# A fused attention and feed-forward kernel: the written-out order of its steps replaced by another, from the 110th step on

## The chip, the cores and the metric

The kernel runs on one core of one Trainium2 chip. The metric is the device time of one execution in microseconds (us); the runs shown give a median of three.

## The reference

Per batch of 8, with 8 heads, 576 rows, head size 64 and 32 memory slots, then a feed-forward layer over all 4,608 rows:

```python
a = softmax(phi, axis=2)                       # over the 576 rows
k_m = einsum('bhsm,bhsd->bhmd', a, k);  v_m = einsum('bhsm,bhsd->bhmd', a, v)
attn = softmax(q @ k_m.T / sqrt(64), axis=-1)  # 576 x 32 per head
x = (attn @ v_m)                               # -> 4608 x 512
out = leaky_relu(x @ w_in, 0.01) @ w_out       # 512 -> 2048 -> 512, float32
```

The two weight matrices lie in memory as float64, the other inputs and the output as float32.

## The kernel before

`v_m` is multiplied into `w_in` ahead of time (a *fold*), so that the feed-forward layer reads the attention weights directly. Products are made of fp16 pairs, high and low part, three matmuls for each product.

The kernel is a dictionary of named steps and a list that says in which order they are issued. The list has 2,188 entries and 2,180 different steps: a few idle products at the start (`z.f`, `z.1`, `z.2`) are run more than once. The list is in two strings, `OPENING` and `LATER`:

```python
    with tc.manual_schedule(engines={ENG.PE, ENG.DVE, ENG.Activation, ENG.Pool, ENG.SP}):
        run(OPENING.split())
        run(LATER.split())
```

Each engine, and the queue of DMAs that SyncE issues, works through its own steps in the order of this list, and a step waits where what it reads is not ready or the buffer that it writes is not free. No step passes an earlier one of its own engine. The names:

- `i0` to `i3`, `o0` to `o3`: quarters of `w_in` and `w_out`. `ld` loads, `h`, `y`, `t` turn 64-bit words into float32, `k` and `l` split into high and low fp16 parts, `s`, `m`, `n` make sums of blocks of `w_out`, `b` sums squares. `ci.1` to `ci.4` and `co.1` to `co.4` derive scales from them; `ci.2`, `co.2` are four small VectorE instructions (lines 494 to 501), `ci.3`, `co.3` one small product each that waits for them (line 507).
- `a0` to `a7`: attention of a batch. `phi`, `kv`, `q0`, `q1` load; `A` and `B` are the softmax over `phi` (`B10`, line 724, subtracts the maximum on VectorE); `C`, `D` make `k_m`, `v_m` and their transposes (`D3` copies the scaled transpose on ScalarE); `Q` transposes queries; `E1` makes scores on TensorE, `E20` to `E23` transpose them on VectorE (line 1120); `S01` to `S08` are the softmax of the scores and its split into fp16 parts, of which `S01` (line 1143), `S02`, `S04` to `S06` and `S08` (line 1207) are VectorE's for batches 2 to 7.
- `Wbj.p` folds quarter j of `w_in` for batch b (line 1242); `h` splits off the high part on ScalarE, `l` the low part on VectorE (line 1281). `w1.1` is `W10.p`.
- `u0` to `u7`: the first 384 rows, in float32: `P` up (line 1340), `V` leaky ReLU on ScalarE, `O` down (line 1411, three products of 512 columns). `P8` to `P15`, with `V`, `C`, `L`, `O`: the next 384 rows, in fp16.
- `p0` to `p59`: the remaining 3,840 rows in 15 groups of 256 rows by four quarters of the hidden size. `p` makes one of four 128 x 256 blocks of the hidden layer (line 1453), two halves of one PSUM bank in turn, so that a `p` step needs the `v` step (leaky ReLU, ScalarE, lines 1472 and 1474) of the block two before. `s` (lines 1488 to 1490) makes four sums of blocks on VectorE; `c.0`, `c.1` cast to fp16 on ScalarE (line 1494), `l.0`, `l.1` make the low parts on VectorE (line 1498). `d.0` to `d.6` are seven products of six matmuls (line 1521); `d.0`, `d.1`, `d.6` read what `l.0` wrote, the other four what `l.1` wrote.
- `x2` to `x15` combine the seven products of a group on VectorE (`x.p` on ScalarE; `x.3` is line 1541), `z` scales and stores, `end` does both for the last group in pieces.

Of the kernel before, what the change touches and what calls it, by code (L numbers as in the profile page):

```python
# [82 lines left out]
o2.m2 o2.s3 V15.0 o2.l2 a3.phi C14 O12.0 V15.1 p0.0 o2.m3 o3.k0 v0.0 o3.k2 O12.1 i2.k1 p0.1 o3.s0
C15 p0.2 L14 O13.0 i3.k1 o3.s1 v0.2 a2.q1 a3.A1 a2.Q1 v0.1 L15 a2.E1 p1.0 i2.l1 o3.s2 o3.l0 a2.E21
a2.E22 o3.k1 p0.3 o3.m0 O13.1 v0.3 o3.l1 v1.0 o2.n2 a2.E20 p1.1 c0.0 o2.n3 i2.k2 a3.A2 a2.D2 o3.l2
a2.D11 o3.n0 p1.2 v1.2 O14.0 v1.1 s0 a2.E3 a2.D4 o3.m3 p1.3 a3.A4 o3.m2 a2.E23 c0.1 O14.1 a2.D5 v1.3
O15.0 l0.0 p2.1 o3.m1 a2.S01 O15.1 c1.0 a2.S02 v2.1 o3.n1 a2.S03 Z1.0 l0.1 o3.n3 p2.0 Z1.2 a2.D6
v2.0 a3.A3 o3.n2 d0.0 d0.1 p2.2 d0.5 a3.kv s1 l1.0 p2.3 a2.S04 Z1.1 c1.1 d0.6 d1.1 d1.0 a3.B10 v2.3
v2.2 i2.l2 p3.0 c2.0 i3.k2 W20.p v3.0 d0.3 l2.0 l1.1 d2.1 p3.1 i3.k0 a2.S05 d0.4 a2.S06 v3.1 d1.5 s2
d1.3 a3.B20 d1.6 p3.3 W20.h0 i3.l0 p3.2 a2.S07 W20.l0 a2.S08 d2.0 d0.2 v3.2 a3.C10 W20.h1 v3.3 c3.0  # L90
d1.4 W20.l1 p4.1 i3.l1 d2.6 c2.1 d1.2 a3.B3 l2.1 v4.1 a3.C2 a3.C30 p4.3 p4.0 d2.3 s3 d2.4 a3.C3k
a3.C31 a4.phi a3.q1 a3.q0 l3.0 v4.0 c3.1 a3.C4 a3.D10 p4.2 W21.p d2.2 l3.1 d2.5 v4.2 v4.3 s4 d3.5
W21.h0 d3.0 W21.h1 W21.l0 c4.0 W21.l1 d3.3 l4.0 p5.1 x2.p W22.p p5.0 c4.1 i3.l2 W22.h1 a3.Q1 W22.h0
# [11 lines left out]
l10.1 s11 v12.1 a4.E1 d10.5 a4.C4 os2 a4.E20 v12.0 p12.3 d8.4 c11.0 d9.4 v12.3 p12.2 l11.0 os3 c11.1
a4.E21 p13.1 d9.6 d10.4 a4.D2 v13.1 a4.E22 a5.A1 v12.2 W32.p p13.3 W32.h0 p13.0 l11.1 d10.6 W32.h1
s12 d11.6 c12.0 d10.2 d9.3 W32.l1 W32.l0 v13.3 v13.0 W33.p p13.2 d10.0 a4.D4 d10.1 d11.0 z3.1 d11.2
a4.D11 c12.1 v13.2 d11.1 a5.A2 l12.1 a4.D5 p14.1 p14.0 l12.0 s13 d10.3 W33.h1 c13.0 a4.E23 v14.0
a5.A4 a5.kv v14.1 W33.l1 d11.3 d11.5 x4.p W33.h0 a4.D6 p14.3 p14.2 x4.0 c13.1 W40.p d11.4 v14.2
l13.0 l13.1 v14.3 W33.l0 W40.h1 c14.0 d12.0 d12.5 p15.1 s14 c14.1 x4.1 a5.A3 x4.2 p15.0 d12.6 v15.1  # L110
d12.3 x4.3 W40.l1 W40.h0 p15.3 l14.1 v15.0 d12.1 d13.1 p15.2 z4.0 os4 v15.2 v15.3 a5.B10 c15.0
a5.B20 d12.2 d13.5 a4.S01 d13.2 p16.1 l14.0 W41.p d13.0 d12.4 v16.1 l15.0 p16.0 d14.0 a4.S02 v16.0
z4.1 a4.S03 d14.2 p16.3 p16.2 d13.6 s15 W41.h0 a4.S04 d13.3 v16.2 d14.1 v16.3 p17.1 c15.1 W40.l0
l15.1 W41.h1 W41.l0 p17.0 v17.1 v17.0 d15.0 d13.4 d14.3 s16 p17.2 d14.4 p17.3 a5.C10 a5.B3 v17.3
v17.2 d14.6 p18.1 c16.1 c16.0 a4.S05 W41.l1 a6.phi l16.0 l16.1 p18.0 d15.2 v18.1 v18.0 c17.0 d14.5
s17 d15.4 a5.C2 x5.p a5.C30 c17.1 d15.1 p18.2 p18.3 d15.5 a4.S06 v18.2 d15.3 x5.0 a4.S07 l17.1 p19.0
# [6 lines left out]
d19.3 d20.0 d19.1 d19.2 v22.1 p22.3 s21 x6.0 c21.0 x6.1 x6.2 c21.1 d19.5 l21.0 W43.p v22.3 a6.A3
a5.D2 v22.2 p23.0 c22.0 x6.3 p23.1 v23.1 d21.0 d20.3 v23.0 d20.5 a5.D4 a5.S01 W43.h1 d20.4 p23.2
l22.0 p23.3 l21.1 v23.2 a5.D11 d20.1 a5.D5 s22 d22.0 p24.0 d20.2 c22.1 v23.3 W43.h0 d20.6 z6.1
W43.l1 c23.0 p24.1 a5.S02 v24.0 d21.2 l22.1 v24.1 d21.4 d22.4 a5.D6 p24.2 v24.2 d21.5 z6.0 d21.6
a5.S03 W50.p p24.3 d22.2 s23 v24.3 d21.1 p25.0 p25.1 c23.1 c24.0 d22.1 l23.0 d23.0 d23.1 a6.B10
l23.1 v25.0 v25.1 p25.3 v25.3 s24 a6.B20 d21.3 d23.2 p25.2 p26.1 v25.2 d22.3 W43.l0 c24.1 x7.p d22.6
# [1606 lines left out]
```

## Time and profile before

| | us |
|---|---|
| median of three runs | 647.3 (645.9 to 648.1) |
| the profiled execution | 647.4 |
| its span, first to last instruction | 645.6 |
| TensorE (PE) busy | 630.3 |
| VectorE (DVE) busy | 529.7 |
| ScalarE (ACT) busy | 402.9 |

[...] "Busy" is the union of the instructions' records. A record of a pipelined matmul is longer than the distance to the next one, so that consecutive records overlap, and a short wait between two matmuls can be hidden by the first one's record.

### The profile page before, as it was taken

The page shows a single profiled execution, that of the slowest core. Times are in us where ns is not written, and L with a number is a line of the kernel's source. Part 1 is how long each engine was busy: PE and PEld are TensorE (multiplying, and loading weights), DVE is VectorE, ACT ScalarE, POOL GpSimd, SP SyncE. Part 2 cuts the span into 40 slices and gives each one's busy share as a digit, 9 for nine tenths or more (in the row PEclk, how much of TensorE's full clock was granted, in tenths as well). Part 3 has the DMA queues.
Part 4 walks back from the last instruction along what each step waited for, and adds up shares of the span by engine and source line. Part 5 has one row for each costly group of instructions (what it writes and reads, how often), then busy time and mean ns, then how long its engine had stood idle before and what let it go on. Part 6 is the DMA issues. An engine that isn't in the chain of part 4 may idle for free.

```text
span 645.6 us, 17428 instructions
## 1 busy us (share of the span) xinstructions
PE 630.3 (98%) x7437; PEld 496.7 (77%) x7437; DVE 529.7 (82%) x841; ACT 402.9 (62%) x699; POOL 14.3 (2%) x34
## 2 busy tenths in 40 slices
...
DMA packets 85404, 61.16 MB, mean 95 GB/s; under 512 B 61648, under 2 KB 68560, under 8 KB 85328
## 3 DMA queue, kind: packets, MB, share of 16 engines
...
q10 hardware_dynamic: 576, 0.56, 0.3%
...
## 4 chain that ended last, share of the span: by engine, by line
PE 52%; DVE 6%; SPq 3%; issue 1%; ACT 1%; DMA 0%; DVEq 0%; ACTq 0%
PE po L1521 27%; PE ph L1453 17%; PE ph L1521 4%; SPq L621 3%; PE pa L1242 2%; DVE arena L1498 1%; DVE arena L986 1%; PE pa L794 1%; DVE r1k L656 1%; PE pa L1044 1%; DVE arena L1488 1%; SPq L1394 0%; DMA arena<-in_q_dram 0%; DVE arena L1489 0%; DVE t L1120 0%
## 5 line engine op out<-in xcount | busy, mean ns | idle before, releaser
L1521 PEld LDWEIGHTS <-arena 128*128 128x128 f16 x2520 | 242.0, 98 | 38.2 <-issue 8.5
L1453 PE MATMUL ph<-a,w_mem 128*128 128x256 f16 (+3 forms) x1656 | 157.0, 243 | 1.0 <-ACT wi L1472 0.7
L1521 PE MATMUL po<-wo,arena 128*128 128x256 f16 x1080 | 139.6, 273 | 1.0 <-DVE arena L1498 0.6
L1521 PE MATMUL po<-arena 128*128 128x256 f16 x1080 | 140.0, 273 | 0.0
L1453 PEld LDWEIGHTS <-w_mem 128*128 128x128 f16 x1656 | 128.6, 98 | 14.8 <-issue 4.6
L1474 ACT ACTIVATE wi<-ph,g_scs 128x256 f32<-128x256 f32 x112 | 53.0, 473 | 82.7 <-PE ph L1453 72.9
L1472 ACT ACTIVATE wi<-ph,g_scs 128x256 f32<-128x256 f32 x112 | 52.9, 472 | 66.1 <-PE ph L1453 64.1
L1498 DVE TENSOR_TENSOR arena<-arena 128x1024 f16<-128x1024 f32 (+1 forms) x58 | 69.9, 1205 | 28.2 <-ACT arena L1494 28.2
L1411 PE MATMUL po<-wo,arena 128*128 128x512 f16 (+1 forms) x240 | 77.1, 467 | 0.8 <-DVE wo L424 0.8
L1494 ACT CAST arena<-arena 128x1024 f16<-128x1024 f32 (+1 forms) x58 | 60.2, 1037 | 21.8 <-DVE arena L1490 17.7
L1498 DVE TENSOR_TENSOR arena<-wi,arena 128x768 f16<-128x768 f32 x56 | 52.9, 948 | 6.0 <-ACT arena L1494 5.9
L1521 PE MATMUL ph<-wo,arena 128*128 128x256 f16 x360 | 48.8, 273 | 0.4 <-DVE arena L1498 0.4
L1494 ACT CAST arena<-wi 128x768 f16<-128x768 f32 x56 | 46.6, 831 | 3.4 <-PE po L1521 2.9
L1488 DVE TENSOR_TENSOR arena<-wi 128x512 f32<-128x512 f32 x56 | 38.5, 687 | 8.5 <-ACT wi L1472 4.3
L1340 PE MATMUL ph<-a,w_mem 128*128 128x192 f16 (+1 forms) x232 | 38.0, 313 | 0.0
L1411 PEld LDWEIGHTS po<-wo,arena 128*128 128x128 f32 x96 | 17.4, 190 | 20.2 <-issue 18.4
L1281 DVE SCALAR_TENSOR_TENSOR w_mem<-pa,w_mem 128x512 f16<-128x512 f32 x40 | 26.9, 681 | 7.0 <-ACT w_mem L1275 7.0
L1242 PE MATMUL pa<-wi,vT 64*32 64x512 f16 (+1 forms) x704 | 29.5, 420 | 0.7 <-DVE w_mem L1281 0.7
L1275 ACT ACTIVATE w_mem<-pa 128x512 f16<-128x512 f32 x40 | 23.1, 598 | 8.1 <-PE pa L1242 2.9
L1490 DVE TENSOR_TENSOR arena<-wi,arena 128x256 f32<-128x256 f32 x56 | 23.8, 425 | 2.0
L1453 PE MATMUL ph<-a,arena 128*128 128x256 f16 (+3 forms) x216 | 24.9, 237 | 0.5 <-ACT wi L1472 0.5
L1489 DVE TENSOR_TENSOR arena<-wi,arena 128x256 f32<-128x256 f32 x56 | 23.8, 425 | 1.9
...
## 6 DMA issues: line engine op xcount, KB each, us to landing
...
```

The costliest lines, as they stand in the source:

```text
L1242: nc.tensor.matmul(pf[g][cols, :], lhs, rhs, start=(n == 0), stop=(n == len(passes) - 1), tile_position=(g * D, hh * M),)
L1281: nc.vector.scalar_tensor_tensor(tiles(t[:, 1]), w(g), ws, tiles(t[:, 0]), ALU.mult, ALU.subtract)
L1340: nc.tensor.matmul(ph[:, t0:t0 + n], lhs, rhs, start=(m == 0), stop=(m == len(seq) - 1))
L1411: nc.tensor.matmul(po, lhs, rhs, start=(f == 0 and m == 0), stop=(f == NQ * NF - 1 and m == len(seq) - 1),)
L1453: nc.tensor.matmul(ph[:, t0:t0 + n], lhs, rhs, start=(m == 0), stop=(m == len(seq) - 1))
L1472: nc.scalar.activation(dst, ph, AF.Prelu, scale=g_sc2n[:, j:j + 1], alpha=1.0 / SLOPE)
L1474: nc.scalar.activation(dst, ph, AF.Prelu, scale=g_sc2[:, j:j + 1], alpha=SLOPE)
L1488: nc.vector.tensor_tensor(gt[:, 0:2], two, gf[:, 1:3], ALU.subtract)
L1489: nc.vector.tensor_tensor(gt[:, 2], gf[:, 1], gt[:, 1], ALU.subtract)
L1494: nc.scalar.copy(dst[:, 0], src)
L1498: nc.vector.tensor_tensor(dst[:, 1], src, dst[:, 0], ALU.subtract)
L1521: nc.tensor.matmul(acc, g[:, x, s, u], rhs, start=(h == 0 and j == 0 and u == 0 and m == 0), stop=(j == NQ - 1 and u == 1 and m == 2), ski ...
```

## The change

The two strings are replaced from their 110th entry on (the first 110 entries, up to `u0.V0 u1.P0`, stay). Both lists hold the same steps, each as often; no step's code changes. The change is described as a new search for an order for 15 whole groups in which dependent operations of an engine are taken to run one behind the other, and loads to land later. The lines that the text below speaks of, in the order of the list; the rest is of the same kind:

```diff
-i1.y0 i1.t0 u0.P1 u1.V0 a0.S11 o0.h0 o0.y0 o0.h1 o1.ld1 i1.h2 i2.ld1 a0.S12 o1.ld2 o0.t0 o0.y1 o0.t1
...
-a1.B10 a0.S16 a1.B20 a1.q0 o0.b o2.t2 u4.V0 o1.b o2.b a1.B3 a1.C10 i3.ld1 a1.Q0 a1.C2 a1.C30 u5.P0
-a1.C31 u2.O1 a1.C4 i3.ld0 a1.Q1 i3.ld2 i3.h1 a1.C3k o3.ld2 a1.D11 i2.b a1.D5 a1.D10 a1.D2 u3.O1
-a1.D4 i3.y1 u4.V1 i3.t1 a1.D3 a1.E1 u5.V0 i3.y0 i3.h0 i3.y2 i3.t0 u4.O0 i3.h2 o3.y2 i3.t2 a1.E22
-u5.P1 a1.E20 i3.b a1.S01 a1.E21 a1.S02 f03.1 ci.1 u5.O0 a2.phi o3.h2 a1.S11 a0.S17 o3.ld1 o3.t2
-u5.V1 o3.y1 a1.S03 ci.2 a2.kv2 a1.S12 a0.S18 o3.h1 u4.O1 a2.A1 a1.S04 a1.S13 o3.t1 ci.3 f03.2 a2.A2
-ci.4 o3.ld0 e. w1.1 o3.h0 o3.y0 W00.h0 a1.S05 a1.S06 o3.t0 u6.P0 u7.P0 a1.S14 W10.h0 u6.V0 o0.s0
-W00.h1 a2.A4 o3.b u7.V0 u6.O0 W00.l0 o0.s1 W00.l1 co.1 a1.S07 W01.h0 a2.A3 a2.B10 co.2 u7.P1 W10.h1
-u6.P1 a2.kv0 co.3 a1.S08 i0.k1
+o0.h0 i1.y2 u1.P1 o0.y0 u1.V0 o0.t0 i1.y0 u0.P1 u0.O0 a0.S11 o0.h1 i1.t0 a0.D2 o1.ld1 i1.h1 o0.y1
...
+a1.C30 a1.C3k a1.D10 i3.ld2 a1.C31 a1.C4 i2.b a1.Q1 u4.P0 a1.D2 i3.h1 a1.D11 i3.y1 a1.D3 u3.O1 a1.D4
+a1.D5 u5.V1 i3.y0 o3.ld2 u4.V0 a1.E1 i3.t1 u4.O0 i3.y2 i3.h0 u5.P0 a0.S16 i3.t0 a1.E20 i3.h2 o3.h2
+a2.phi o3.y2 a1.E21 i3.t2 i3.b o3.ld1 a1.S01 u5.V0 a1.E22 f03.1 o3.ld0 ci.1 a1.S02 f03.2 a1.S11
+o3.t2 a1.S12 a2.A1 a1.S13 u5.O0 a1.S03 w1.1 o3.h1 ci.2 a0.S17 a2.A2 o3.y1 ci.3 a1.S04 ci.4 e. a1.S14
+u6.P0 o3.y0 o3.h0 o3.t1 o3.t0 W00.h1 u7.P0 u4.O1 W10.h0 W00.h0 W00.l1 u6.V0 u6.O0 a1.S05 o0.s0
+W00.l0 o0.s1 a0.S18 W10.h1 a1.S06 o3.b W01.h1 co.1 a1.S07 W10.l1 u7.V0 a1.S15 u6.P1 a2.A4 a1.S08
+W10.l0 W11.p co.2 W01.l1 W01.h0 co.3
...
-d4.2 z2.0 c6.0 a3.E1 s6 a3.E23 a3.E21 p7.3 p7.2 z2.1 a3.E22 v7.3 d4.6 l6.0 c6.1 a3.E20 d5.5 d5.4
-W30.p a4.A3 v7.2 p8.1 a4.B10 l6.1 d5.6 d6.0 c7.0 a3.S01 v8.1 p8.0 s7 W30.h0 W30.l0 c7.1 d5.3 d5.2
...
-d8.5 p11.1 a4.C30 p11.0 d9.0 a4.C31 l9.1 v11.0 a3.S08 v11.1 a4.Q0 c10.0 x3.3 d9.1 s10 l10.0 a4.C3k
-d8.2 p11.2 d9.5 v11.2 d8.6 p12.0 p11.3 z3.0 a4.Q1 a4.D10 d8.3 a5.phi c10.1 v11.3 a4.D3 d9.2 p12.1
...
-a6.A1 a6.A2 a4.S08 a5.E20 d17.4 a5.E21 c20.0 d18.6 a5.E23 d17.5 p21.0 p21.1 d18.4 a5.E22 l19.0 a6.A4
...
-l59.0 d58.0 d59.0 end.p l59.1 d58.2 d57.5 d59.2 d59.3 d59.6 d59.4 d58.5 d59.5 end.0 end.1 d57.1
-d58.1 end.2 end.3 end.z1 d59.1 end.4 end.z2 end.5 end.z0
...
+v3.3 d1.4 a3.C10 W20.l1 c2.1 v3.2 p4.0 p4.1 v4.0 a3.C2 l2.1 i3.l1 a3.C30 i3.k2 s3 v4.1 d2.4
...
+d5.3 a3.E21 d5.4 a3.E23 v7.3 p8.0 c7.0 a3.E20 l7.0 p8.1 W30.p d6.6 c6.1 d7.1 d7.0 a4.kv a4.B20 l6.1
+v8.0 W30.h0 v8.1 p8.3 a3.E22 s7 W30.h1 W30.l1 c7.1 p8.2 v8.3 v8.2 d7.6 c8.0 d5.5 a3.S01 l7.1 d5.2 s8
...
+v11.0 v11.1 d9.0 z3.0 a3.S07 p11.3 p11.2 v11.3 d8.4 l10.0 a4.D10 d9.6 a3.S08 d9.3 v11.2 a4.Q1 p12.0
...
+d20.5 d21.4 v23.3 d20.6 a4.S08 v23.2 p24.0 p24.1 c22.0 W42.h1 l22.0 d21.0 c23.0 c22.1 v24.0 d22.0
...
+d57.0 l58.1 s59 d57.2 c59.0 d58.0 d58.3 d58.4 d58.5 d57.6 l59.0 d59.0 d58.6 d58.2 c59.1 l59.1 d59.2
+d59.4 d59.3 end.p d59.6 end.0 d59.5 end.1 d57.1 end.2 d58.1 d59.1 end.4 end.3 end.z2 end.z1 end.5
+end.z0
```

## Rows read from the trace of the kernel before

**Rows 1.** The page's busy time, share and instruction count of each engine.

```profile
PE 630.3 (98%) x7437; PEld 496.7 (77%) x7437; DVE 529.7 (82%) x841; ACT 402.9 (62%) x699; POOL 14.3 (2%) x34
```

**Rows 2.** Windows: busy us (x instructions) by engine, clock, DMA share, GB/s.

```profile
45.00:100.00 55.00, 53.11 (x448) 26.06 (x447) 46.80 (x91) 47.90 (x74) 8.75 (x8) 1.00 0.63 199
100.00:150.00 50.00, 50.00 (x538) 31.27 (x537) 49.47 (x68) 42.73 (x70) 2.12 (x4) 1.00 0.34 76
150.00:275.00 125.00, 122.25 (x1763) 99.54 (x1760) 120.40 (x194) 75.37 (x137) 0.20 (x2) 1.00 0.39 102
275.00:300.00 25.00, 25.00 (x394) 21.92 (x393) 22.09 (x32) 15.12 (x25) 0.00 (x0) 1.00 0.14 39
300.00:500.00 200.00, 198.60 (x2493) 171.16 (x2490) 166.41 (x263) 115.00 (x211) 0.10 (x1) 1.00 0.29 66
500.00:600.00 100.00, 100.00 (x1099) 88.85 (x1099) 71.21 (x103) 56.40 (x99) 0.00 (x0) 1.00 0.07 17
600.00:645.60 45.60, 41.47 (x380) 36.92 (x378) 23.81 (x36) 18.75 (x33) 0.00 (x0) 1.00 0.14 36
```

**Rows 3.** TensorE's timeline: waits; in brackets idle time before and releaser.

```profile
70.00 1.93 PE L1088 MATMUL pa<-arena,kT 32*32 32x192 f32 x96 [0.74 <-ACT kT L937]
...
92.81 0.38 PE L507 MATMUL pa<-diag,ones 4*128 4x4 f32 x2 [1.08 <-DVE diag L501]
...
154.63 0.33 PE L915 MATMUL pa<-ident,x_v 128*128 128x128 f32 x1 [0.24 <-DVE t L1120]
...
263.89 0.84 PE L1242 MATMUL pa<-wi,vT 64*32 64x512 f16 x23 [0.23 <-DVE w_mem L1281]
...
349.27 0.49 PE L1453 MATMUL ph<-a,arena 128*128 128x256 f16 x3 [0.53 <-ACT wi L1472]
```

**Rows 4.** VectorE's timeline: two instructions of an `s` step, and the next.

```profile
236.48 0.42 DVE L1489 TENSOR_TENSOR arena<-wi,arena 128x256 f32<-128x256 f32 x1
236.94 0.42 DVE L1490 TENSOR_TENSOR arena<-wi,arena 128x256 f32<-128x256 f32 x1
237.28 0.68 DVE L1281 SCALAR_TENSOR_TENSOR w_mem<-pa,w_mem 128x512 f16<-128x512 f32 x1
```

**Rows 5.** Opening, from three views: `u3.O1`; `a2.B10` and `co.2`; folds of batches 0, 1.

```profile
66.52 2.74 PE L1411 MATMUL po<-wo,arena 128*128 128x512 f32 x6
...
89.39 1.96 DVE L724 TENSOR_TENSOR arena<-arena,r1k 128x1152 f32<-128x1152 f32 x1
...
91.28 0.27 DVE L494 TENSOR_REDUCE m<-pa 4x1 f32<-4x128 f32 x1
...
91.94 0.82 DVE L501 TENSOR_SCALAR diag<-ident,m 4x4 f32<-4x4 f32 x1
...
L1242 PE MATMUL pa<-wi,vT 64*32 64x512 f32 x128 | 8.7, 601 | 0.0
```

**Rows 6.** Groups of instructions by form, VectorE: `l`, `a.E2`, `a.S01`.

```profile
L1498 DVE TENSOR_TENSOR arena<-arena 128x1024 f16<-128x1024 f32 x56 | 68.0, 1215 | 28.2 <-ACT arena L1494 28.2
...
L1120 DVE STREAM_TRANSPOSE t<-pa 128x512 f32<-128x512 f32 x12 | 8.3, 700 | 1.3 <-PE pa L1044 1.3
...
281.40 1.34 DVE L1143 TENSOR_REDUCE tm<-t 128x36 f32<-128x1152 f32 x1
```

**Rows 7.** Timelines of TensorE and VectorE: a `d` step, `d9.1`, and `x3.3`.

```profile
243.09 0.82 PE L1521 MATMUL ph<-wo,arena 128*128 128x256 f16 x6
243.75 0.82 PE L1521 MATMUL po<-wo,arena 128*128 128x256 f16 x6
...
246.72 0.65 DVE L1541 TENSOR_TENSOR obs<-obs,po 128x512 f32<-128x512 f32 x1
```

**Rows 8.** Timelines of VectorE and TensorE: `a4.S08` and `p24.0`.

```profile
320.62 1.42 DVE L1207 TENSOR_TENSOR a<-t,a 128x1024 f16<-128x1024 f32 x2
...
346.61 0.49 PE L1453 MATMUL ph<-a,arena 128*128 128x256 f16 x3
```

**Rows 9.** Timeline of the end: the last combination.

```profile
641.51 0.48 DVE L1568 SCALAR_TENSOR_TENSOR obs<-po,scales,obs 128x256 f32<-128x256 f32 x1 [1.02 <-PE po L1521]
```

More of the change, by code (lines that the diff above doesn't have):

```diff
@@ L83 @@
[L83 to L93, printed above, removed]
@@ L105 @@
[L105 to L116, printed above, removed]
@@ L123 @@
[L123 to L128, printed above, removed]
@@ new lines @@
+P8.0 a2.A3 o0.s2 o0.n1 W11.l1 i0.k1 o0.m2 u5.O1 o0.k1 o0.s3 V8.0 o0.n2 o0.k0 W11.l0 o0.l2 a2.kv3
+V9.1 P8.1 o0.l1 a2.kv0 i0.l2 i1.k0 i0.l1 P9.0 o1.s0 o0.m3 u6.O1 W02.h0 o0.n3 V8.1 W02.h1 W02.l0
+o0.l0 V9.0 o1.k2 W12.p W02.l1 o1.l2 C8 C9 o1.s1 o1.m0 P10.0 W12.h0 W12.h1 i1.k1 L8 W12.l1 V10.0
+u7.O1 o1.n0 P10.1 Z0.2 a2.B10 W12.l0 Z0.1 V10.1 Z0.0 C10 L9 o1.m1 i1.l1 o1.n1 o1.k0 P11.0 V11.0
+o1.l0 W13.p o1.s2 P11.1 O8.0 V11.1 C11 W03.h1 W03.h0 P12.1 O8.1 L10 a2.B20 V12.1 P13.1 W03.l1 o1.s3
+P12.0 W03.l0 i1.l0 L11 o1.m2 o1.k1 a1.S16 V12.0 o1.l1 O9.0 o1.n2 W13.h0 i2.k0 W13.l0 o2.k0 a1.S17
@@ new lines @@
+v1.2 O14.0 o3.m0 o3.l2 o3.m3 o3.n0 s0 v1.1 a2.E21 a2.E3 O14.1 p1.3 p2.0 a2.E20 o3.m1 a2.D2 o3.n1
+a2.D11 v1.3 a2.E23 O15.0 o3.n2 a2.S01 v2.0 c0.1 o3.n3 p2.1 a2.S02 c1.0 O15.1 a2.D4 v2.1 i2.l2 d0.0
+l0.1 p2.2 a2.D5 a3.kv p2.3 l1.0 Z1.1 Z1.2 Z1.0 d0.3 i2.l1 a2.D6 a3.B10 a2.S03 d0.5 W20.p s1 v2.2
+v2.3 d0.1 p3.0 a2.S04 i3.k0 p3.1 d0.2 d0.6 c1.1 d1.1 a3.B20 d1.6 l1.1 v3.0 d1.3 d0.4 a2.S05 c2.0
+l2.0 v3.1 a2.S06 d1.0 d2.1 s2 a2.S07 p3.2 i3.l0 d2.0 W20.h0 d1.5 W20.l0 a2.S08 p3.3 d1.2 d2.6 a3.B3
+W20.h1 v3.3 d1.4 a3.C10 W20.l1 c2.1 v3.2 p4.0 p4.1 v4.0 a3.C2 l2.1 i3.l1 a3.C30 i3.k2 s3 v4.1 d2.4
@@ new lines @@
+c9.0 p10.3 d7.5 x3.0 d8.5 s9 a4.C2 c9.1 d8.6 a3.S04 x3.1 v10.0 v10.3 l9.0 x3.2 p11.1 d8.1 p10.2 d8.2
+a3.S05 v10.2 l9.1 d9.1 a3.S06 p11.0 a4.C30 d9.5 d9.2 W31.l1 x3.3 c10.0 s10 d8.3 a4.C3k a4.C31 a5.phi
+v11.0 v11.1 d9.0 z3.0 a3.S07 p11.3 p11.2 v11.3 d8.4 l10.0 a4.D10 d9.6 a3.S08 d9.3 v11.2 a4.Q1 p12.0
+c11.0 p12.1 d10.0 a4.Q0 a4.C4 c10.1 l11.0 a4.D3 v12.0 d10.1 a4.E1 l10.1 a4.E22 v12.1 a4.E20 d11.0
+s11 p12.2 p12.3 d11.1 v12.2 d10.3 d10.6 v12.3 c11.1 c12.0 p13.0 p13.1 a4.E21 v13.1 l12.0 W32.p v13.0
```

177 lines of the change are left out of this document (96 added, 81 removed).

## Prediction

> **What bounds the kernel now.** I read the page's busy times first [rows 1]: TensorE is busy for 630.3 of 645.6 us, VectorE for 529.7, ScalarE for 402.9. So no reordering can give more than TensorE's 15.3 us of idle time and what its records hide, and the question is where that idle time lies. The windows [rows 2] answer it: the first 45 us are ahead of the 110th step and stay as they are; of the rest TensorE is idle for 55.00 - 53.11 = 1.89 us up to 100, 0 up to 150, 2.75 from 150 to 275, 0 up to 300, 1.40 from 300 to 500, 0 up to 600, and 4.13 in the last stretch. In those windows the VectorE column tells why: from 100 to 275 it is idle for only 0.53 + 4.60 us, after 500 for 28.8 of 100.
>
> TensorE's timeline then names the waits [rows 3]: two in 45 to 150 (ScalarE's `a1.D3`, VectorE's chain `co.2`); eight in 150 to 275, of which the first and the last are shown, seven ended by VectorE and one by ScalarE; four small ones after 300. A product's record lasts 0.27 us, but six of them start every 0.66 us, 0.109 apart [rows 7], so a wait hides 0.164 us more than it shows. All that can be won between 45 and 600 us is 1.89 + 2.75 + 1.40 + 14 x 0.164 = 8.3 us. The last stretch is not won by order: TensorE ends, one combination of 0.48 us follows [rows 9], then a store; both orders end with `d59.1`, `end.5` and `end.z0`. The new one issues `end.z2` and `end.z1` together shortly ahead of it; I take nothing for that.
>
> The sum is made against the profiled execution, 647.4 us (span 645.6 and 1.8 around it), which is 0.1 above the median of the runs, 647.3. About 0.3% (1.9 us) is what a measurement here can tell from no change.
>
> **The change part by part.** No instruction is added or removed: the list's 2,188 entries come in another order, each engine and the DMA queue in list order. What is priced is cover: the TensorE work that stands between a step and the TensorE step that needs it.
>
> *Opening.* `a1.E1` stood directly behind `a1.D3` and waited 0.74 us, hidden part included 0.90. Now `u3.O1` stands between, 2.7 us of products [rows 5], so the wait goes: -0.9. `co.3` waited 1.08 because `a2.B10` (1.96 us) held up `co.2` on VectorE [rows 5]. `a2.B10` now comes later, but `co.2` (91.28 to 92.76, 1.48 us) stands behind the fold `W11.p`, and nothing of TensorE stands behind that before `co.3`. A fold of this batch is 8.7 / 8 = 1.09 us, so 0.39 of the wait stays: -0.7. `ci.3` loses the `u4.O1` that covered `ci.2` and gets the same place behind the fold `w1.1`: +0.4. Together -1.2; the bounds are -2.2 (1.89 + 2 x 0.164, every wait of this stretch) and +1.5 (neither saving comes, and `ci.3` waits for the whole of its chain).
>
> *150 to 275 us.* Here I counted, in both orders, what VectorE has ahead of the same TensorE step. Ahead of `p8.0` the new order has dropped `a3.E20` (0.70), `l6.1` (1.22) and `a3.S01` (1.34) [rows 6], with nothing of VectorE put in: 3.3 us less. Ahead of `p12.0` VectorE's work is the same, but six more product steps (`d9.2 d8.3 p11.3 d8.4 d9.6 d9.3`), 6 x 0.66 = 3.9 us, stand there for TensorE. So VectorE gets 3 to 4 us more time where it had 5 us of idle time in 175 [rows 2]. How late it was shows at `x3.3`: the old list has it directly ahead of `d9.1`, which TensorE began at 243.75, and VectorE reached it at 246.72, 2.97 us later [rows 7]. A cause is in the rows of `s`: the second half-sum needs the first and starts 0.04 us after its end, the next instruction, which needs neither, starts 0.08 us before the end [rows 4]. A plan that lets every VectorE instruction follow alike is thus late by some 0.1 us at each dependent one, and the change is said to plan for this.
>
> [...]
>
> The eight waits here are 2.75 + 8 x 0.164 = 4.1 us. The relief of 3 to 4 us is as large as the lateness, but relief at some steps makes others tight: in both orders many `l` steps stand directly ahead of a `d` step that reads them (`l2.1` and `d2.4` now). I take two thirds, -2.7; the bounds are 0 and -4.1.
>
> *After 275 us.* What is put off must come later. `a4.S08`, the last step of batch 4's attention, was done from 320.62 to 322.04, and `p24.0`, the first to need it, began at 346.61 [rows 8]: 24.6 us of cover. Now it stands directly ahead of `p24.0`. Its 1.42 us and some 0.1 to the next engine are covered at least by the `d20.6` (0.65) that runs when it starts: +0.9; bounds 0 (VectorE ahead of the list) and +0.9 + 3.0 (as late as `x3.3`). The four waits after 300, 1.4 + 4 x 0.164 = 2.1 us, I leave as they are: the new order has as many places of their kind (a `p` step two products behind the `v` step that frees its half bank).
>
> *Later landings.* Loads move a few steps in a list whose DMA queue waits for buffers most of the time; no TensorE wait of rows 3 ends on a DMA. 0.
>
> Sum: -1.2 - 2.7 + 0.9 = -3.0, so 647.4 - 3.0 = 644.4.
>
> **The rivals.**
>
> *The waits move.* VectorE stays busy for 97% or so of 100 to 275, and what is won at `p8.0` is lost at the next tight place. For it: the tight `l`, `W` and `S08` places are about as many in the new list. Against it: 3 to 4 us is more than any single wait there. Time: 647.4 - 1.2 + 0.9 = 647.1.
>
> [...]
>
> *Slower: batch 4 arrives late.* Place: `a4.S08` ahead of `p24.0`, where nothing but the running product covers. If VectorE is still as late there as at `x3.3`, 2.97 us, and the stretch before keeps its waits, the time is 647.4 - 1.2 + 0.9 + 3.0 = 650.1. It decides from a lateness of 1.9 + 1.2 - 0.9 = 2.2 us on. For it: rows 7 and 8. Against it: VectorE has idle time again after 275 (2.9 us in 25) to catch up.
>
> *More than forecast.* All waits of 150 to 275 and half of those after 300 go, and VectorE is ahead at `p24.0`: 647.4 - 1.2 - 4.1 - 1.0 = 641.1.
>
> **How the numbers follow.** Forecast 644.4: 0.45. More than forecast, 641.1: 0.05. The waits move, 647.1: 0.27. The rule on dependent steps, 647.1: 0.03. Slower, 650.1: 0.20. The first two are faster by over 0.3% (0.50), the next two within it (0.30), the last slower (0.20). The range reaches from 640.8, just below the larger gain and short of the 639.1 at which every wait is gone, to 650.0, which cuts off only the slower case's upper half. As both signs hold chance, the forecast's own range stands beside it: 643.7 to 645.8, half of the way from its -2.7 to each bound of the part from 150 to 275 us.
>
> **What the changed profile would show.** `a1.E1` starts without idle time behind `u3.O1`; `co.3` and `ci.3` wait under 0.6 us each. In the window that holds `p4` to `p13` TensorE's idle time falls from 2.75 to about 1 us, and VectorE's busy share drops from 96% to 95% or less. `p24.0` waits about 0.7 us for `a4.S08`'s line. TensorE's busy time itself barely moves, by the hidden parts of the waits that went, 1 to 2 us; the clock stays at 1.00. The prediction is wrong if TensorE's waits on VectorE lines between 150 and 350 us come to as much as now, or if `p24.0` waits over 2 us. It is right for the wrong reason if the gain lies after 350 us or in the last stretch.

## The result, and the profile after

The new order takes 640.1 us (median of six executions, 639.7 to 641.7), the one before 647.7 beside it (six, 645.9 to 649.7): ratio 0.9886, 95% interval 0.9866 to 0.9906. That is 7.6 us less, where 3.0 was forecast. The profiled execution took 640.72 us, span 638.5.

Of the 114 executions of the kernel before whose clock this study has, 40 have a mean granted clock of 0.996 or 0.997 and a median of 648.6 us, 74 one of 0.998 or more and 646.1; of the 45 timed executions of the new order and of the lists below that share its opening and get no long wait of their own from the edit, none is under 0.998. So 6.0 us is what the order gives at full clock (646.1 - 640.1); over all 114 the median before is 646.7, and the rest of the 7.6 is clock that it loses in a third of its executions, and chance in six of them.

The page of the kernel after, busy times (for [rows 1]; its line numbers are one higher than before):

```profile
PE 628.6 (98%) x7437; PEld 497.3 (78%) x7437; DVE 530.2 (83%) x841; ACT 403.0 (63%) x699; POOL 14.9 (2%) x34
```

The windows of the kernel after, for [rows 2]:

```profile
45.00:100.00 55.00, 53.84 (x450) 26.69 (x449) 46.86 (x92) 48.94 (x76) 7.46 (x7) 1.00 0.65 205
100.00:150.00 50.00, 49.70 (x555) 31.87 (x554) 49.22 (x70) 43.92 (x73) 2.53 (x5) 1.00 0.35 79
150.00:275.00 125.00, 125.00 (x1800) 103.07 (x1798) 120.91 (x193) 74.93 (x135) 0.20 (x2) 1.00 0.40 104
275.00:300.00 25.00, 25.00 (x382) 21.92 (x380) 21.43 (x31) 16.01 (x27) 0.00 (x0) 1.00 0.13 29
300.00:500.00 200.00, 200.00 (x2548) 172.99 (x2546) 171.89 (x268) 115.03 (x209) 0.10 (x1) 1.00 0.27 65
500.00:600.00 100.00, 100.00 (x1066) 89.09 (x1064) 69.63 (x102) 57.81 (x102) 0.00 (x0) 1.00 0.09 23
600.00:638.50 38.50, 34.56 (x317) 30.73 (x315) 20.15 (x31) 15.02 (x26) 0.00 (x0) 1.00 0.11 28
```

From 150 to 600 us TensorE has no idle time at all, where it had 2.75 and 1.40 us. VectorE is as busy as before from 150 to 275 (120.91 us, 120.40 before) and busier from 300 to 500 (171.89, 166.41 before): the same total of work, with some of it put later against TensorE's. The last stretch is as it was (3.94 us idle, 4.13 before).

TensorE's timeline from 45 to 600 us has these waits and no other, for [rows 3]:

```profile
58.58 2.52 PE L795 MATMUL pa<-arena 64*32 64x128 f32 x144 [0.27 <-ACT arena L731]
87.23 2.81 PE L1412 MATMUL po<-wo,arena 128*128 128x512 f32 x6 [0.90 <-DVE wo L425]
128.79 0.64 PE L795 MATMUL pa<-arena 64*32 64x128 f32 x25 [0.29 <-issue]
```

Idle time that a record hides counts too. A sum that holds it: the start of a step less TensorE's own work ahead of it in the list (each entry at the distance its matmuls keep undisturbed), taken at landmarks of both traces.

| TensorE's time lost, us | before | after | difference |
|---|---|---|---|
| up to `u0.P0` (the same entries) | 3.48 | 4.27 | +0.8 |
| `u0.P0` to `P8.0` | 5.10 | 4.14 | -1.0 |
| `P8.0` to `p0.0` | 0.36 | 0.95 | +0.6 |
| `p0.0` to `p16.0` (150 to 275 us) | 7.39 | 2.21 | -5.2 |
| `p16.0` to `d59.1` | 4.68 | 2.53 | -2.2 |

Together -7.0, and the spans differ by 7.1. The first line is no effect of the change: over the profiled executions of this study it lies between 3.2 and 4.3 in lists of either kind. The last line is at the upper end: by the same sum new_192_old, new_90_old, old_b10_later and old_pool_later, which follow the order of before from `p16.0` on, lose 0.9 to 1.6 us more there than the new order, not 2.2. So the profiled execution before, 647.4 us, is longer than the 646.1 of full clock, and the two traces differ by more than 6.0.

### The profile page after: what moved, and what is told of

The parts are those of the page before. It is cut to its first block, busy times and chain, and to the rows that moved or that the text cites. A ratio compares the mean times of both kernels' runs of the same rounds, so it can differ in the third digit from the quotient of the medians.

```text
span 638.5 us, 17410 instructions
## 1 busy us (share of the span) xinstructions
PE 628.6 (98%) x7437; PEld 497.3 (78%) x7437; DVE 530.2 (83%) x841; ACT 403.0 (63%) x699; POOL 14.9 (2%) x34
## 4 chain that ended last, share of the span: by engine, by line
PE 94%; DVE 3%; ACT 1%; DMA 1%; issue 1%; POOL 0%; DVEq 0%; POOLq 0%
PE po L1522 37%; PE ph L1454 25%; PE po L1412 11%; PE ph L1522 6%; PE ph L1341 5%; PE pa L1243 4%; PE pa L795 2%; PE pa L1045 1%; PE po L1638 1%; DMA arena<-in_moe_w_out_dram 1%; DVE wo L425 0%; PE pa L363 0%; ACT wi L430 0%; PE pa L1089 0%; DVE wo L725 0%
## 5 line engine op out<-in xcount | busy, mean ns | idle before, releaser
L1454 PE MATMUL ph<-a,w_mem 128*128 128x256 f16 (+3 forms) x1656 | 154.9, 243 | 0.0
L1522 PE MATMUL po<-arena 128*128 128x256 f16 x1080 | 137.9, 273 | 0.0
```

Source lines behind the costliest of these rows:

```text
L1454: nc.tensor.matmul(ph[:, t0:t0 + n], lhs, rhs, start=(m == 0), stop=(m == len(seq) - 1))
L1522: nc.tensor.matmul(acc, g[:, x, s, u], rhs, start=(h == 0 and j == 0 and u == 0 and m == 0), stop=(j == NQ - 1 and u == 1 and m == 2), ski ...
```

## The experiments

Each was timed against the kernel before on the same chip. "Full clock" is the median of the executions with a mean granted clock of 0.998 or more, with their count and, behind the bar, that of the kernel before on that chip.

| run | median us | ratio, 95% interval | under 0.998 | full clock, run / before |
|---|---|---|---|---|
| old_to_p0 | 644.67 | 0.9963 (0.9942 to 0.9983) | 6 of 12 | 642.8 / 646.0 |
| old_to_p16 | 645.23 | 0.9990 (0.9977 to 1.0004) | 2 of 12 | 645.1 / 646.0 |
| new_to_p16 | 645.44 | 0.9981 (0.9962 to 1.0000) | 6 of 12 | 644.2 / 646.0 |
| old_192_new | 642.91 | 0.9932 (0.9908 to 0.9956) | 3 of 6 | 641.8 / 646.7 |
| new_192_old | 644.89 | 0.9960 (0.9940 to 0.9979) | 0 of 11 | 644.9 / 646.7 |
| new_90_old | 644.89 | 0.9967 (0.9952 to 0.9981) | 0 of 12 | 644.9 / 646.1 |
| old_patched | 645.70 | 0.9985 (0.9970 to 0.9999) | 0 of 12 | 645.7 / 646.0 |
| old_free_s | 642.60 | 0.9926 (0.9901 to 0.9951) | 0 of 6 | 642.6 / 646.7 |
| new_free_s | 640.16 | 0.9887 (0.9864 to 0.9909) | 0 of 5 | 640.2 / 646.7 |
| new_slow_s | 641.86 | 0.9912 (0.9892 to 0.9932) | 0 of 6 | 641.9 / 646.1 |
| old_s08_late | 647.85 | 1.0009 (0.9991 to 1.0027) | 6 of 12 | 647.4 / 646.1 |
| old_b10_later | 645.94 | 0.9985 (0.9973 to 0.9998) | 0 of 12 | 645.9 / 645.9 |
| old_pool_later | 645.27 | 0.9977 (0.9964 to 0.9990) | 0 of 12 | 645.3 / 645.9 |
| new_u6_later | 643.00 | 0.9931 (0.9909 to 0.9953) | 5 of 6 | 641.0 (one) / 646.1 |
| new_s14_later | 640.14 | 0.9896 (0.9878 to 0.9914) | 0 of 5 | 640.1 / 645.9 |
| old_loads2 | 650.29 | 1.0054 (1.0035 to 1.0073) | 7 of 12 | 649.4 / 645.8 |

**Where in the list.** Six lists follow one order up to a step and then issue what is left in the other order. The seams:

```diff
 # old_to_p0: before, then after
 C14 O12.0 V15.1 p0.0
-o2.m3 o3.k0 v0.0
+p0.1 v0.1 v0.0
 # old_to_p16: before, then after
 v16.1 l15.0 p16.0
-d14.0 a4.S02 v16.0
+W40.l0 d14.0 W41.h1
 # new_to_p16: after, then before
 c14.1 p16.1 p16.0
-a4.S02 d13.2 v16.0
+os3 W40.h1 a5.A3
 # old_192_new: before, then after
 d2.5 v4.2 v4.3
-s4 d3.5 W21.h0
+d3.1 W21.h1 d3.0
 # new_192_old: after, then before
 d3.1 a3.C4 l3.1
-W21.h1 d3.0 d3.4
+s4 d3.5 W21.h0
 # new_90_old: after, then before
 W01.h1 co.1 a1.S07
-W10.l1 u7.V0 a1.S15
+a2.kv2 a2.A4 u7.V0
```

> The old list up to p0.0 (143 us), the rest in the new list's order. Reading the two profiles by TensorE work done, the new list gains nothing ahead of p0.0 (-0.4 us), 5.1 us from there to p16.0 and 2.2 us after it. If the gain lies where VectorE is crowded and not in the opening: 7.4 us under the kernel before, TensorE without a wait from 150 to 600 us. If the opening or earlier loads set up the gain: at least half of it missing, 3.5 us or less under the kernel before.

> The old list up to p16.0 (286 us), the rest in the new order. If the waits after p16.0 (four in the profile of before) go by the new order itself: 2.2 us under the kernel before. If they were a debt of VectorE from the crowded stretch, which this list still has: 0 to 1 us under it.

> The new list up to p16.0 (280 us), the rest in the old order. If the stretch up to p16.0 gives its 4.7 us by itself: 4.7 us under the kernel before, and the old list's four waits after p16.0 are back. If those waits were a debt from before p16.0, they stay away: 7 us under it.

> The old list up to its v4.3 (192 us), then the new order. There the two lists have the same steps behind them but for l3.1, so that the seam brings no wait of its own. By the two profiles the old list has lost 1.8 us more of TensorE's time than the new one up to here, and 5.1 us more after it. If the gain is made where the waits were: 5.1 us under the kernel before, no TensorE wait after 195 us. If it needs the new list from the opening on (loads placed earlier, VectorE ahead): 2 us or less under it, with waits on VectorE after 195 us.

> The new list up to its l3.1 (190 us), then the old order; the counterpart. If the gain is made where the waits were: 1.8 us under the kernel before, and the old list's waits at W33.p, d8.5 and p12.1 are back. If the new opening puts VectorE ahead for good: 5 us or more under it.

> The new list up to `a1.S07` (about 90 us), then the remaining steps in the order of before: the opening alone. The prediction's term for it is -1.2 us. The new trace, in which the waits that went from `a1.E1`, `co.3` and `ci.3` came back at `u6.O0` and two others, says 0, within 0.7 of the kernel before, if the seam brings no wait of its own.

Two seams spoil their own run: behind `p0.0` the joined list waits 0.93 and 1.75 us (148.18 and 151.43), behind `p16.0` of new_to_p16 2.88 us (286.10), so these two give less than their half is worth, and half of new_to_p16's executions lose clock. The others are clean. At full clock the new opening alone is worth 1.2 us (new_90_old), the new list up to 192 us 1.8, and the new list from there on 4.8 (old_192_new, 646.7 - 641.8); old_to_p16 has all eight waits of 150 to 275 us and none behind, so the waits after 300 us go by the order there and are no debt of the earlier ones; its 0.9 us are not clear of noise (0.9977 to 1.0004). Most of the gain lies from 192 us on. For new_90_old I expected 0, because the new list waits at `u6.O0`; here that wait is absent. The GpSimd multiplication that causes it (`a1.S15`, at 84.27 us in the kernel after, below) stands behind the seam, and there behind `a1.S08`, so the 1.2 us are those of an opening without this wait.

**VectorE's pace.** In old_free_s and new_free_s the second and third instruction of each `s` step no longer read what the one ahead wrote; two of the four half-sums are therefore other sums, the work is the same. In new_slow_s each `s` step gets a fifth instruction.

```diff
 # old_free_s, new_free_s
-        nc.vector.tensor_tensor(gt[:, 2], gf[:, 1], gt[:, 1], ALU.subtract)
-        nc.vector.tensor_tensor(gt[:, 3], gf[:, 3], gt[:, 2], ALU.subtract)
+        nc.vector.tensor_tensor(gt[:, 2], gf[:, 1], gf[:, 2], ALU.subtract)
+        nc.vector.tensor_tensor(gt[:, 3], gf[:, 3], gf[:, 2], ALU.subtract)
 # new_slow_s
         nc.vector.tensor_tensor(gt[:, 3], gf[:, 3], gt[:, 2], ALU.subtract)
+        nc.vector.tensor_tensor(gt[:, 3, 0:8], gf[:, 3, 0:8], gt[:, 2, 0:8], ALU.subtract)
```

> The old list; the second and third of the three VectorE instructions of each s step read gf alone, no longer the sums written just before, so that no instruction of s depends on another (sums of other blocks are formed: that part of the computation is changed). Spacing goes from +0.04 to -0.08 us, some 0.12 us at two places in each of 60 steps, 3.4 us of VectorE's time from 150 to 275 us. If VectorE's lateness by such spacing makes the waits: at least half of the 4.1 us of that stretch go, 2 to 5 us under the kernel before. If the spacing does not matter: within 1 us of it.

> The new list with the same change to the s steps (that part of the computation is changed). Its TensorE waits for nothing from 150 to 600 us, so both theories expect no change: within 0.7 us of the new kernel, 640.1. If it gets faster by more, TensorE is held up by VectorE in a way that its waits don't show.

> The new list with a fifth, very short VectorE instruction in each of the 60 `s` steps (it writes the first 8 columns of the last sum again, with the same values, and depends on the instruction ahead of it). By the nearest rows it costs 0.15 to 0.3 us of VectorE's time, so 9 to 18 us in all, about as much as the two dependences that were taken out of the old list. If the new list gains because it was made with VectorE's real time and has little room beyond it, most of the gain goes: +2 to +5, 642 to 645. If it gains because its steps stand better whatever VectorE's pace, it stays within 0.7 of 640.1.

VectorE's timeline of old_free_s, an `s` step's last two instructions and the next; and its window of 150 to 275 us:

```profile
245.39 0.41 DVE L1489 TENSOR_TENSOR arena<-wi 128x256 f32<-128x256 f32 x1
245.72 0.42 DVE L1490 TENSOR_TENSOR arena<-wi 128x256 f32<-128x256 f32 x1
246.06 0.95 DVE L1498 TENSOR_TENSOR arena<-wi,arena 128x768 f16<-128x768 f32 x1
```

```profile
150.00:275.00 125.00, 124.61 (x1814) 102.59 (x1802) 121.15 (x201) 77.85 (x140) 0.20 (x2) 1.00 0.40 105
```

Of the same length, they start 0.33 us apart instead of 0.46 [rows 4], and with nothing else changed TensorE's idle time in that window falls from 2.75 to 0.39 us and that of 300 to 500 us from 1.40 to 0; the time falls by 4.1 us at full clock. 60 steps with two such places are some 15 us of VectorE's time that the order before had not provided for. The new list gains nothing from the same relief (640.16), and loses 1.8 us when 9.3 us are added to VectorE (539.5 us busy, 530.2 without; ratio 0.9912 against 0.9886, on another chip). The 1.8 lies between the two expectations (+2 to +5, and within 0.7): VectorE's pace matters to the new list too, and it has some room. That it has this room because its plan counted the dependent steps is what the change is said to do, and no run tests it.

**Mending the waits one by one.** old_patched is the list of before with the thirteen steps that TensorE waits at after 45 us each moved a few entries later (or what it waits for earlier), two of the moves:

```diff
-u3.O1 a1.D4 i3.y1 u4.V1 i3.t1 a1.D3 a1.E1
+u3.O1 a1.D4 i3.y1 u4.V1 i3.t1 a1.D3
...
-u4.O0 i3.h2
+u4.O0 a1.E1 i3.h2
...
-d8.5 p11.1
+p11.1 d8.5
```

> The old list with 13 of its waits after 45 us treated one by one: the waiting TensorE step, or the VectorE step in front of its producer, is moved behind the next product or two, nothing else. If each wait is a matter of its place alone, nearly all of their 8 us go: 7 to 8 us under the kernel before. If VectorE is behind in the crowded stretch, as the forecast had it, the waits move to the next tight place: 0 to 3 us under it.

Its timeline of TensorE, the waits from 150 to 275 us:

```profile
181.71 2.42 PE L794 MATMUL pa<-arena 64*32 64x128 f32 x142 [0.69 <-DVE w_mem L1281]
195.22 0.37 PE L1242 MATMUL pa<-wi,vT 64*32 64x512 f16 x1 [0.66 <-DVE w_mem L1281]
195.82 0.84 PE L1242 MATMUL pa<-wi,vT 64*32 64x512 f16 x23 [0.22 <-DVE w_mem L1281]
251.48 0.30 PE L1044 MATMUL pa<-arena,x_k 64*32 64x64 f32 x4 [1.23 <-ACT x_k L924]
252.02 0.25 PE L1044 MATMUL pa<-arena,x_k 64*32 64x64 f32 x2 [0.24 <-DVE arena L986]
254.92 0.83 PE L1453 MATMUL ph<-a,w_mem 128*128 128x192 f16 x12 [0.27 <-ACT wi L1474]
```

The waits that were mended are gone and 3.3 us of others have come. While VectorE is behind the list, a wait that is filled comes back at the next step: the rival "the waits move" is right for this edit, and wrong for the new list, in which VectorE is not behind.

**The cover of `p24.0`.** In the list of before `a4.S08`, which stands 89 entries ahead of `p24.0`, is moved to where the new one has it.

```diff
-a6.A1 a6.A2 a4.S08 a5.E20 d17.4
+a6.A1 a6.A2 a5.E20 d17.4
...
-d22.0 p24.0
+d22.0 a4.S08 p24.0
```

> The list of before with one step moved: `a4.S08` goes from 60 entries ahead to the place directly ahead of `p24.0`, as the new list has it. The prediction's term says +0.9 us (only the running product covers its 1.42 us), its slower rival +3.0 or more (VectorE late by as much as at `x3.3`). The reading of the new trace, that VectorE is ahead of the list there and that its 1.42 us are done before TensorE comes, says 0 to +0.5. All against the kernel before.

Timelines of TensorE and VectorE in old_s08_late, and in the kernel after (for [rows 8]):

```profile
345.46 0.38 PE L1453 MATMUL ph<-a,arena 128*128 128x256 f16 x2
346.33 1.42 DVE L1207 TENSOR_TENSOR a<-t,a 128x1024 f16<-128x1024 f32 x2
347.60 0.27 PE L1453 MATMUL ph<-a,arena 128*128 128x256 f16 x1 [1.76 <-DVE a L1207]
```

```profile
339.70 1.42 DVE L1208 TENSOR_TENSOR a<-t,a 128x1024 f16<-128x1024 f32 x2
341.76 0.49 PE L1454 MATMUL ph<-a,arena 128*128 128x256 f16 x3
```

The place itself costs what was feared, a wait of 1.76 us, in a list where VectorE comes 0.9 us after TensorE; in the new list VectorE has ended 0.64 us before. My expectation of 0 to +0.5 for this run was wrong at the wait and close in the time (+0.5, interval -0.6 to +1.7); at full clock it is +1.3, nearer the prediction's +0.9. The price of a place depends on how far VectorE is behind the list there, not on the place.

**The opening: GpSimd, VectorE and the clock.** In the profiled executions of lists that open as the one before, `co.3` waits either 1.0 to 1.1 us or 2.0. The windows of one of the latter kind (old_to_p0, whose first 496 entries are those of before):

```profile
92.00:94.00 2.00, 0.03 (x1) 0.00 (x0) 1.90 (x6) 1.11 (x3) 0.00 (x0) 1.00 0.00 0
94.00:96.00 2.00, 1.99 (x5) 1.07 (x6) 1.97 (x6) 0.07 (x1) 0.00 (x0) 0.83 0.00 0
96.00:98.00 2.00, 2.00 (x4) 0.67 (x2) 2.00 (x3) 2.00 (x4) 0.00 (x0) 0.50 0.01 4
98.00:100.00 2.00, 2.00 (x21) 0.38 (x20) 1.90 (x7) 1.08 (x2) 0.00 (x0) 0.82 0.00 0
```

After TensorE has stood for 1.98 us the granted clock of these windows falls to 0.83, 0.50 and 0.82, and from 100 to 102 us it is 1.00 again. If it was either 1.00 or 0.50 within a window, that is an estimate of 3.4 us at 0.50, where the expectation of old_b10_later (below) has 3.7. Three profiled executions have the long wait, 1.96 to 1.99 us; the clock falls behind it in two (to 0.50 from 96 to 98 us in old_to_p0 and in old_192_new) and stays at 1.00 in the third (old_loads2, 94 to 104 us), so the fall is likely behind such a wait and not certain. It shows behind none of the short ones (1.00 in each 2 us from 86 to 102 in before, old_to_p16, old_free_s and old_s08_late). What makes the wait one or the other, in the timelines of VectorE and GpSimd of the kernel before and of old_to_p0:

```profile
88.97 0.39 DVE L692 TENSOR_TENSOR r1k<-r1k 128x128 f32<-128x128 f32 x1
89.06 1.08 POOL L1207 TENSOR_TENSOR a<-t,a 128x384 f16<-128x384 f32 x1 [6.07 <-DVE w_mem L1281]
90.10 2.60 POOL L1160 TENSOR_TENSOR t<-t,ts__886 128x768 f32<-128x768 f32 x1
91.94 0.82 DVE L501 TENSOR_SCALAR diag<-ident,m 4x4 f32<-4x4 f32 x1
```

```profile
89.35 0.99 POOL L1208 TENSOR_TENSOR a<-t,a 128x384 f16<-128x384 f32 x1 [5.85 <-ACT a L1203]
89.49 1.10 DVE L693 TENSOR_TENSOR r1k<-r1k 128x128 f32<-128x128 f32 x1
90.30 1.64 POOL L1161 TENSOR_TENSOR t<-t,ts__886 128x768 f32<-128x768 f32 x1
90.62 2.53 DVE L725 TENSOR_TENSOR arena<-arena,r1k 128x1152 f32<-128x1152 f32 x1
93.74 0.22 DVE L502 TENSOR_SCALAR diag<-ident,m 4x4 f32<-4x4 f32 x1
```

Where VectorE starts 0.09 us ahead of GpSimd, its instruction takes 0.39 us and GpSimd's two take 1.08 and 2.60. Where GpSimd is 0.14 us ahead, GpSimd's take 0.99 and 1.64, and VectorE's 1.10 and 2.53 (0.39 and, in [rows 5], 1.96): 1.3 us that `co.2` comes later. old_192_new and old_loads2 have GpSimd ahead too (by 0.11 and 0.13), and VectorE's two take 1.11 and 2.53 there, and 1.10 and 2.53. In these rows, of two instructions that run at the same time, the one that starts second takes longer than elsewhere (a collision, below); why, no trace says. `a2.B10` ends 1.21 us behind the end of a GpSimd instruction both times (93.15 behind 91.94 in the second fence; 91.35 in [rows 5] behind 90.14 in the first). The 4x4 instruction is longer beside GpSimd too: in the first fence it takes 0.82 us instead of 0.22 and ends at 92.76, just behind GpSimd's end at 92.70. Two edits of the list before, and two of the new one, act on this:

```diff
 # old_b10_later
-co.1 a1.S07 W01.h0 a2.A3 a2.B10 co.2 u7.P1
+co.1 a1.S07 W01.h0 co.2 a2.A3 a2.B10 u7.P1
 # old_pool_later
-co.1 a1.S07 W01.h0 a2.A3 a2.B10 co.2 u7.P1 W10.h1 u6.P1 a2.kv0 co.3 a1.S08 i0.k1
+co.1 W01.h0 a2.A3 a2.B10 co.2 u7.P1 W10.h1 u6.P1 a2.kv0 co.3 i0.k1 a1.S07 a1.S08
 # new_s14_later
-a1.S14 u6.P0 o3.y0 o3.h0 o3.t1 o3.t0
+u6.P0 o3.y0 o3.h0 o3.t1 o3.t0 a1.S14
 # new_u6_later
-u6.V0 u6.O0 a1.S05
+u6.V0 a1.S05
...
-u6.P1 a2.A4
+u6.P1 u6.O0 a2.A4
```

> The list of before with two VectorE steps of batch 2, `a2.A3` and `a2.B10`, moved from directly ahead of `co.2` to directly behind it. Theory: in the list of before `co.3`'s wait is 1.0 to 1.1 us where VectorE starts ahead of GpSimd and 2.0 where GpSimd starts first, and after the wait of 2.0 TensorE's granted clock falls to 0.50 for about 3.7 us. Then this edit takes the wait away, no execution has a mean granted clock under 0.998, and the time is 1 to 1.5 below the full-clock executions of before (646.1), so 644.7 to 645.2, and 2 to 2.5 below the median of before. Rival: the loss of clock comes from another place, and a third of the executions still show it.

> The list of before, VectorE's order untouched: ScalarE's `a1.S07`, whose result GpSimd waits for, moved behind `i0.k1`, with GpSimd's `a1.S08` behind it, so that GpSimd starts some 3 us later, when `co.2` is done. Theory (the two engines hold each other up where they run at the same time): VectorE's short last instruction of `co.2` takes 0.2 instead of 0.8 us, `co.3` waits about 0.5 us instead of 1.1 or 2.0, and no execution has a mean clock under 0.998: 0.6 below the full-clock executions of before, 1.5 below its median. Rival (VectorE's chain is late by itself): `co.3` waits as before, and a third of the executions still lose clock.

> The new list with `a1.S14` (VectorE, three short instructions whose result starts a GpSimd multiplication of 2.0 us) moved behind `o3.t0`. In the new trace `o3.t0` takes 2.24 us beside that multiplication, its twin `o3.t1` 0.90, and `u6.O0` waits 0.90 us for it. If the two engines hold each other up, `o3.t0` takes 0.9, the wait goes, and the time is 0.3 to 1.0 below the new list (640.1), the rest lost where GpSimd's multiplication falls next. If `o3.t0` is slow by itself, nothing changes.

> The new list with one step moved: `u6.O0`, which waits 0.90 us of TensorE's time for `o3.t0` at 87.23 us, goes behind `u6.P1`, some 3 us of products later. If that wait is a place of its own, 0.9 to 1.1 us go and the time is about 639.1 against 640.1 for the new list. If the products behind it need VectorE as late as it does (VectorE is idle for only 8 of the 55 us up to 100), the wait comes back at another step and the time stays at 640.

With `a2.B10`'s collision gone, or moved behind `co.2`, no execution of either edit of the old list loses clock (0 of 24, beside 9 of 23 of the kernel before on that chip). old_pool_later, which leaves VectorE's order alone, gains the 0.6 us expected at full clock: `a2.B10` takes 1.36 us and `co.3` waits 0.32. Its 4x4 instruction takes 0.72 all the same: GpSimd has started at 91.66, ahead of it (91.87). old_b10_later takes `co.3`'s wait away but gets one of 0.62 us at 106.05, and at full clock nothing is left of the expected 1.0 to 1.5.

In the new list the same collision sits at `o3.t0`. The timelines of the kernel after and of new_s14_later, the two conversions `o3.t1` and `o3.t0` in one row (x2), GpSimd's multiplication, and what follows:

```profile
84.04 3.04 DVE L425 SCALAR_TENSOR_TENSOR wo<-arena 128x768 uint32<-128x768 uint32 x2
84.27 2.00 POOL L1161 TENSOR_TENSOR t<-t,ts__864 128x768 f32<-128x768 f32 x1 [1.90 <-DVE ts__864 L1158]
```

```profile
81.48 1.82 DVE L425 SCALAR_TENSOR_TENSOR wo<-arena 128x768 uint32<-128x768 uint32 x2
84.85 1.77 POOL L1161 TENSOR_TENSOR t<-t,ts__871 128x768 f32<-128x768 f32 x1 [3.64 <-DVE ts__871 L1158]
85.19 1.97 DVE L460 TENSOR_TENSOR arena<-wo 128x512 f32<-128x512 f32 x1
89.70 0.58 PE L1243 MATMUL pa<-wi,vT 64*32 64x512 f32 x1 [0.53 <-DVE arena L1282]
```

The pair takes 1.82 instead of 3.04 us and `u6.O0`'s wait is gone, but the sum that now meets GpSimd takes 1.97 (0.68 before), and a fold waits 0.53 us. 640.14 us is no gain over 640.1: the collision was moved. new_u6_later missed: with `u6.O0` out of the way the step behind it waits for the same late `o3.t0` by way of ScalarE, and longer:

```profile
88.64 0.27 PE L490 MATMUL pa<-ident,sq 128*4 128x128 f32 x1 [2.83 <-ACT wi L430]
```

Behind that wait the clock is at 0.50 from 90 to 92 us, and five of six executions end under 0.998. `u6.O0` was the cover of that step.

**Loads.** In old_loads2 18 loads of batches 2 to 7 are moved toward their places in the new list, as far as the readers of their buffers allow (old_loads moves loads farther, past such readers, so that its 679 us are of another computation). The move that decides:

```diff
-a4.q0 a4.q1
+a4.q1
...
+a4.q0
```

> The list of before with 18 of the 27 loads of batches 2 to 7 moved toward where the new list has them, by 0.4 to 3.7 us of TensorE's work, as far as the steps that read their buffers before and after allow; all else in the order of before. The prediction's term for the landings is 0: within 0.7 us of the kernel before, with the eight waits from 150 to 275 us still there. If the landings carry part of the gain, 1 us or more and some of those waits gone.

> The list of before with the loads of batches 3 to 7 moved to where the new list has them, by the TensorE work ahead of them (two that would come behind their first reader stay). The prediction's term for the landings is 0, and neither trace shows a TensorE wait behind a DMA after 45 us: within 0.7 us of the kernel before. If the landings carry part of the gain, 1 us or more.

VectorE's timeline in old_loads2:

```profile
251.55 1.38 DVE L986 STREAM_TRANSPOSE arena<-arena 128x1152 f32<-128x1152 f32 x1 [3.05 <-DMA arena<-in_q_dram]
```

Neither expectation held: 3.9 us slower. `a4.q0`, which lands at 241.42 us in the kernel before, came so late that VectorE's `a4.Q0` starts at 251.55 instead of 245.43; the list still had it first, and VectorE stood for 3.05 us in the stretch where it has none to spare; TensorE lost 1.95 and 1.49 us behind it. The new list has `Q1` ahead of `Q0` to match and reads `a4.q0`, which lands at 247.06, at 247.82. The landings can't be moved apart from the steps that read them; that they gain nothing by themselves is argued (no wait on a DMA in TensorE's timeline of before or after), not shown. The DMA queue of the kernel before waits for some 456 of 645.6 us, but some 290 of them at the stores of the output, for what they are to write: not for buffers most of the time, as the prediction has it.

## Why the prediction was wrong, point by point

**The stretch from 150 to 275 us** is the step that failed: "I take two thirds, -2.7". All eight waits went, and with what records hide TensorE lost 5.2 us less between `p0.0` and `p16.0`. The cause that the prediction named is the right one: old_free_s shows that the dependent steps' time made the order before late, by the gain that came when it was taken away. What was wrong is the discount. I reasoned that relief at some steps makes others tight; that holds while VectorE is behind the list (old_patched), but the new list keeps it ahead. Over 200 to 275 us the `s` and `l` steps and `x3.3` (29 in each trace) start on average 1.15 us before the TensorE step that stands next in the list, where they started 0.08 us after it (0.26 before it in old_free_s). The new list has `x3.3` seven entries behind `d9.1`; it starts 1.15 us after it, and 1.47 us ahead of the TensorE step that follows it in the list (`d8.3`, 243.29). In the order before it came 2.97 us after the one that follows it [rows 7]:

```profile
240.67 0.71 PE L1522 MATMUL po<-wo,arena 128*128 128x256 f16 x5
241.82 0.68 DVE L1542 TENSOR_TENSOR obs<-obs,po 128x512 f32<-128x512 f32 x1
```

The bound of -4.1, too, was short of the 5.2: 0.164 us hidden for each shown wait leaves out waits that no record shows. The count ahead of `p8.0` was incomplete without harm: the new order also puts `a3.E22` (0.70 us) behind it, and `W30.p` (0.77 us of TensorE's time), so the relief there is 3.2 us where 3.3 were taken.

**After 275 us**, the second failed step: "The four waits after 300 [...] I leave as they are", and +0.9 at `p24.0`. The waits went, 2.2 us from `p16.0` on in the two traces and 0.9 to 1.6 by the other four; old_to_p16 and old_free_s lose them too, the one by the order there, the other by VectorE's pace. `p24.0` waited for nothing. The +0.9 was a fair price for the place in the order before (1.76 us of wait there, +1.3 in the time). Its 0.1 us to the next engine was an estimate; at `co.3` 0.05 us lie between VectorE's end (92.76) and TensorE's start (92.81) [rows 3] [rows 5].

**The opening**, -1.2, is near the 1.0 us of the two traces, and new_90_old measures 1.2 at full clock, but the terms are not the ones summed, so the match is in part luck: `a1.E1`, `co.3` and `ci.3` start without any wait, where 0.39 and 0.4 us were left to the last two, and in the new list `u6.O0` waits 0.90 instead. The 1.48 us of `co.2` and 1.96 of `a2.B10` in [rows 5] were not VectorE's own time: 0.6 us of each goes with GpSimd's work beside it (`a2.B10` takes 1.36 in old_pool_later, the 4x4 instruction 0.22 in old_to_p0). What was not seen at all is that the order before loses clock in a third of its executions, most likely behind this wait: some 0.9 us on the mean (40 of 114 times 2.5).

**The rivals.** "The waits move" is shown for single edits and wrong for the list as a whole. No run shows the term "rule on dependent steps" (647.1, at 0.03). What the runs show: rows 4 have 0.12 us between the spacings of an instruction that depends on the one ahead and one that does not, and with the dependence taken out in old_free_s it is 0.33 us from start to start against 0.46, and the ratio 0.9926 (0.9901 to 0.9951). "Batch 4 arrives late" is right that the place costs something in the order before, but 1.76 us of wait where it priced 3.9, and in the new order it did not happen. "More than forecast", 641.1 us at a chance of 0.05, was the nearest.

**The signs named in advance.** Right: `a1.E1`, `co.3`, `ci.3`; TensorE's busy time 1.7 us less; the clock of the profiled execution. Wrong: about 1 us of idle time left from 150 to 275 (0), VectorE's share there down to 95% (96.7%), 0.7 us at `p24.0` (0).
